# Three banks of scores in the first visit of each batch's first pair, the fourth bank behind the value products: local attention woven into a bilinear feed-forward on one NeuronCore

## The chip, the cores and the metric

The kernel runs on one core of one Trainium2 chip. The metric is the device time of one launch in microseconds (us). The time before is 975.85 us, the median of three runs (973.68 to 976.51).

## The reference

Eight batches of eight heads, 576 positions and head dimension 64 go through attention with a causal window of 128 and a linear distance bias; the result, 512 wide per position, goes through a bilinear feed-forward with inner width 1536.

```python
scores = scale * np.matmul(q, k.transpose(0, 1, 3, 2))
bias = slopes[:, None, None] * (-np.abs(rel).astype(np.float32))[None, :, :]
mask = (rel >= 0) & (rel < window)
scores = np.where(mask, scores + bias[None], -1000000000.0)
scores = scores - np.max(scores, axis=-1, keepdims=True)
attn = np.exp(scores)
attn = attn / (np.sum(attn, axis=-1, keepdims=True) + 1e-09)
attn_out = np.matmul(attn, v)
...
a = x @ w_a
b = x @ w_b
return (a * b @ w_out).astype(np.float32)
```

## The kernel before, in words

**Two interleaved streams.** The feed-forward of one batch is the main stream: `up` (two products with the inner weights, some of them as a seven-product scheme, `up_fast`) and then `down` (line 1003, 48 steps of six 128x288 matmuls, each with its own 128x128 weights). The attention of a later batch is a Python generator, `attention()`, that yields seven times per pair of heads; `Pace.along` advances it evenly along the main stream. Batches are numbered 0 to 7 here and pairs of a batch 0 to 3. Pair 0 and pair 1 of batch b run beside `down` of batch b-2, pairs 2 and 3 beside `up` of batch b-1. In the code `i` is the running pair, `p` its place in the batch, `o` the pair whose scores are made, `prev` the pair before it, `nxt` the next one, and `two` is 2 for batches 2 to 7.

**What sets the order.** From batch 1 of the feed-forward on, TensorE's instructions stand in the order in which the code issues them. The other engines' orders, and that of SyncE's queue of DMAs, are set by a scheduler that weighs due times, so a move on TensorE can reorder them too. Each engine then executes its own list strictly in order, waiting on semaphores. A run of attention matmuls between two steps of the main stream is called a visit below.

**One pair of attention.** `scores(o, bi)` makes one of four PSUM banks of scores (line 417: 128x64 weights `qst`, 192 columns; bank 0 holds three 64-row tiles of queries, banks 1 to 3 two each); VectorE adds the bias and takes the minimum (line 422), ScalarE the exponential (line 423) into a tile `t`. `normalize(o)` takes the reciprocal of the row sums (435, 436) and writes the probabilities as a 16-bit high part (ScalarE, 439) and low part (VectorE, 440) into `phl`. `transpose_probs` is one DMA transpose of `phl` into `pT` (445), issued by SyncE once both parts of all banks are there. `pv` multiplies `pT` with the split values `vhl` (541); ScalarE copies the result back over the values `v` (454). There is one buffer each of `phl`, `pT`, `qst`, `qk` and `v`, four of `t`, and three PSUM banks (`ps_at`) for scores, value products and small totals.

**The next pair's layout.** `split_qk(nxt)` and `low_qk(nxt)` split the loaded queries and keys into high (`qkh`, ScalarE 373) and low parts (`qkl`, VectorE 378), scaled by a factor `own` (VectorE 112, 118, 119, 371) that comes from one small matmul `qtot` (367). `lay_out_qk` moves them with four DMAs of SyncE's queue: 385 and 386 copy the upper halves into `qst`, then 387 and 388, which must wait for these to land, move the lower halves. Scores of a pair need all four.

**The values.** When pair 0 of a batch runs, the batch before is finished: `split_x` (POOL 489 to 499, ScalarE 475, VectorE 476) reads the whole of `v` to make the feed-forward's input, `hidden_scale` (TensorE 556, VectorE 557) finds its scale. Only then `load_v` (SyncE 297, 1280 KB) may fill `v` for the new batch, in pair 1. `v_squares` takes its squares, two of four parts on ScalarE (309), two on VectorE (307).

Of the kernel before, what the change touches and what calls it, by code (L numbers as in the profile page):

```python
# [46 lines left out]
def attention_then_bilinear_ffn(ctx: ExitStack, tc: tile.TileContext, qT, kT, vP, w_a, w_b, w_out, rel, slopes2, outT):  # L47
# [245 lines left out]
    def load_v(b):  # L293

        st = State()
        st.v = work.tile([P, NPAIR, VCOLS], F32, tag="v", name="v")
        sp.dma_start(st.v, vP[b])
        st.xq = work.tile([P, S], BF16, tag="xq", name="xq")
        return st
# [49 lines left out]
    def qk_squares(b, p, qk):  # L349
        o = State()  # L350
        o.b, o.p, o.qk = b, p, qk
        sums = small.tile([P, 1], F32, tag="qs", name="qs")
        hi = work.tile([P, 2, S], F16, tag="qkh", name="qkh", bufs=2)
        lo = work.tile([P, 2, S], F16, tag="qkl", name="qkl", bufs=2)
        with tc.issue_after(last_phl[0].ins) if b == 2 and p == 1 else ExitStack():
            act.activation(lo.bitcast(BF16), qk, AF.Square, accum_out=sums)

        o.both = small.tile([P, 2], BF16, tag="both", name="both")
        o.ready = vec.tensor_scalar(out=o.both, in0=halves, scalar1=sums, scalar2=None, op0=ALU.mult)
        o.kh, o.kl = hi, lo  # L360
        return o

    def split_qk(o):

        b, p, qk, hi, lo = o.b, o.p, o.qk, o.kh, o.kl
        tot = ps_at.tile([P, 512], F32, tag="at", name="qtot")
        pe.matmul(tot[:, 0:2], ones16, o.both, start=True, stop=True)
        sc = small.tile([P, 2], F32, tag="sc", name="sc")
        power_scale(sc, tot[:, 0:2], 1.01, 15)
        own = small.tile([P, 3], F32, tag="own", name="own")  # L370
        vec.tensor_tensor_reduce(out=own[:, 0:2], in0=sc, in1=halves, scale=1.0, scalar=0.0, op0=ALU.mult, op1=ALU.add, accum_out=own[:, 2:3])
        own = own[:, 2:3]
        act.activation(hi, qk, AF.Copy, scale=own)
        o.sc, o.own = sc, own

    def low_qk(o, behind=None):
        with tc.issue_after(behind.ins) if behind else ExitStack():
            vec.scalar_tensor_tensor(out=o.kl.rearrange("p h s -> p (h s)"), in0=o.qk.rearrange("p h s -> p (h s)"), scalar=o.own, in1=o.kh.rearrange("p h s -> p (h s)"), op0=ALU.mult, op1=ALU.subtract)
# [17 lines left out]
    def before_scores(o, ninv):  # L396
        o.bias = work.tile([P, WIN], F32, tag="bias", name="bias")
        last_bias[0] = pool.tensor_scalar(out=o.bias, in0=rel_sb, scalar1=ninv, scalar2=sl2_sb[:, o.p:o.p + 1], op0=ALU.mult, op1=ALU.mult)  # L398
        o.mn, o.sm, o.rin = (small.tile([P, 9], F32, tag=tag, name=tag) for tag in ("mn", "sm", "rin"))
        o.n, o.parts = 0, []  # L400
# [26 lines left out]
    def normalize(o):  # L427

        a, z = o.parts[0][0], o.n

        if o.b < 2:
            vec.tensor_scalar(out=o.rin[:, a:z], in0=o.sm[:, a:z], scalar1=1e-9, scalar2=1.0 / PSC, op0=ALU.add, op1=ALU.mult)
        else:

            act.activation(o.rin[:, a:z], o.sm[:, a:z], AF.Copy, scale=1.0 / PSC, bias=1e-9 / PSC)
        vec.reciprocal(o.rin[:, a:z], o.rin[:, a:z])  # L436
        for m, e, pc, w in o.parts:
            s = o.rin[:, m:m + 1]
            beside[0] = last_phl[0] = act.activation(phl[:, 0, pc:pc + w], e, AF.Copy, scale=s)  # L439
            beside[1] = vec.scalar_tensor_tensor(out=phl[:, 1, pc:pc + w], in0=e, scalar=s, in1=phl[:, 0, pc:pc + w], op0=ALU.mult, op1=ALU.subtract)  # L440
        o.parts = []
# [102 lines left out]
    def pv(p, st, o, vhl):  # L544
        xp = new_x_ps()
        hi, lo = o.pT[:, 0:NCOL // P, :], o.pT[:, NCOL // P:2 * NCOL // P, :]
        each_pv(xp, (vhl[:, 0, :], vhl[:, 1, :], vhl[:, 0, :]), (hi, hi, lo))
        keep_x(p, st, xp, 1.0 / PSC)
# [161 lines left out]
    def attention():  # L710


        n = NPAIR * (B - 1)
        qks = {}

        def load(i):
            if i < n:

                qks[i] = (load_plain_qk if i < NPAIR else load_qk)(1 + i // NPAIR, i % NPAIR)

        def squares(i):
            if i >= n:
                return None
            qk = qks.pop(i)
            return qk if i < NPAIR else qk_squares(1 + i // NPAIR, i % NPAIR, qk)

        def split(o, whole=True):
            if o and o.b > 1:
                split_qk(o)
                if whole:  # L730
                    low_qk(o)

        def lay_out(o):
            if o:
                before_scores(o, lay_out_qk(o) if o.b > 1 else -8.0)

        def behind():

            return tc.issue_after(last_read[0].ins) if last_read[0] else ExitStack()

        load(0)
        st, prev = load_v(1), None
        o = squares(0)
        lay_out(o)
        load(1)
        yield 0
        for i in range(n + 1):
            b, p = 1 + i // NPAIR, i % NPAIR

            two = 2 if o and o.b >= 2 else 1  # L750
            if two == 2 and p == 1:
                with behind():
                    nxt = squares(i + 1)
            for bi in range(two if o else 0):
                scores(o, bi, nxt.ready if two == 2 and p == 1 and nxt else None)
            if two == 1 or p != 1:
                with behind():
                    nxt = squares(i + 1)
            if p == 1 and b > 1:
                st = load_v(b)  # L760
            if p == (1 if b == 1 else 2):
                v_scale(st)
            yield i + 1 / 7
            if o and two == 1:
                scores(o, 1)

            if p == 2:

                with tc.issue_after(first_reads[0].ins) if first_reads[0] else ExitStack():
                    late.vhl = split_v(st, late.p)  # L770
            elif prev and p != 1:
                prev.vhl = split_v(st, prev.p)
            yield i + 2 / 7
            if p == 2:
                pv(late.p, st, late, late.vhl)
                transpose_probs(prev)
                split(nxt)
            if o and p != 2:
                with behind():
                    normalize(o)  # L780
            if p != 2:
                split(nxt, p != 3)
            yield i + 3 / 7
            if o:
                scores(o, 2)
            if p == 3 and nxt and nxt.b > 1:
                low_qk(nxt, beside[1])
            if prev and p not in (1, 2):
                pv(prev.p, st, prev, prev.vhl)
            if two == 2 and p in (1, 3):  # L790
                if p == 2:
                    with behind():
                        normalize(o)
                scores(o, 3)
            yield i + 4 / 7
            if p == 2:
                prev.vhl = split_v(st, prev.p)
                if two == 1 or p not in (1, 3):
                    with behind():
                        normalize(o)  # L800
            if o and (two == 1 or p not in (1, 3)):
                scores(o, 3)
            lay_out(nxt)
            load(i + 2)
            if p == (0 if b == 1 else 1):
                v_squares(st, (0, 1))
            if prev and p == 0:
                states[b - 1] = st
                assert started["down"] == b - 2
                for k, _ in enumerate(split_x(st, b - 1 <= 3, b - 1 >= 2)):  # L810
                    yield i + (4.2 + 0.2 * k) / 7
            yield i + 5 / 7
            if o:
                with behind():
                    normalize(o)
            if p == (0 if b == 1 else 1):
                v_squares(st, (2, 3), vec if b > 2 else act)
            yield i + 6 / 7
            if prev and p == 0:
                hidden_scale(st)  # L820
            if p == 2:
                pv(prev.p, st, prev, prev.vhl)
            if p == 1:
                late = prev
            elif o:
                transpose_probs(o)
            prev, o = o, nxt
            yield i + 1
# [305 lines left out]
```

## Time and profile before

| what | value |
|---|---|
| runs before | 973.68, 975.85, 976.51 us |
| the profiled execution's own time | 975.07 us |
| its span, first to last instruction | 973.3 us |
| outside the span | 1.8 us |
| TensorE busy | 958.6 us, 98% of the span |
| VectorE busy | 683.1 us |
| ScalarE busy | 626.3 us |
| POOL busy | 260.7 us |
| mean granted TensorE clock | 0.996 |

A line of the timeline gives start, duration, engine, source line, operation, the tiles written and read, and a count; a bracket gives idle time just before it and what ended that. PE is TensorE, PEld its weight loads, DVE VectorE, ACT ScalarE, SPq SyncE's queue of DMAs. A line of the waits gives the waiting engine and line, what it waited for, the total in us, the number of times and the longest.

### The profile page before, as it was taken

To read this page: it belongs to the slowest core of one execution; us is meant where nothing else is said; L and a number is where in the kernel's file an instruction comes from. 1 tells how busy PE (TensorE), PEld (TensorE's weight loads), DVE (VectorE), ACT (ScalarE), POOL (GpSimd) and SP (SyncE) were. 2 spreads that over 40 slices of the span, in tenths; PEclk is the share of its full clock that TensorE was granted. 3 is DMA by queue.
4 is the path that set the end of the run, shared out by engine and by line. 5 is a ranking of instruction groups with operands and counts; after the bars stand their busy time and mean duration, and the time that the engine had idled before them with its cause. 6 is when DMAs were issued, how large, how long until landed. Compare 5 with 4: busy or idle time off the path is not lost.

```text
span 973.3 us, 23844 instructions
## 1 busy us (share of the span) xinstructions
PE 958.6 (98%) x9340; PEld 747.8 (77%) x9341; DVE 683.1 (70%) x1896; ACT 626.3 (64%) x1701; POOL 260.7 (27%) x307
## 2 busy tenths in 40 slices
PE   8989999999999999999999999999999999999998
PEld 6667777777877777777877777777777778877776
DVE  6999998568888768887777877667676676514520
ACT  6878788577776666776766876767666765423321
POOL 1211122044546123631235222401222122301100
PEclk9999999999999999999999999999999999999999
DMA  9463736635347333464246552464245450210001
GB/s 351 143 259 111 254 84 135 146 102 111 90 97 171 75 69 72 109 158 93 52 92 172 101 104 50 111 177 93 45 94 130 117 100 12 57 37 2 1 13 37
DMA packets 148432, 102.82 MB, mean 106 GB/s; under 512 B 120032, under 2 KB 128352, under 8 KB 147296
## 3 DMA queue, kind: packets, MB, share of 16 engines
q1 hardware_dynamic: 138816, 91.77, 38.5%
q10 hardware_dynamic: 9504, 9.54, 3.1%
q8 instruction: 73, 1.20, 0.5%
q14 instruction: 39, 0.32, 0.1%
HBM read 48.33 MB, written 9.44 MB: 59 GB/s over the span
## 4 chain that ended last, share of the span: by engine, by line
PE 86%; DVE 5%; DMA 4%; ACT 3%; issue 1%; SPq 0%; POOL 0%; ACTq 0%; DVEq 0%
PE dn_ps L1003 23%; PE ch L907 19%; PE up_ps L907 17%; PE p L907 15%; PE x_ps L541 5%; PE sc_ps L417 4%; DMA v<-in_vP 2%; PE dn_ps L869 1%; PE sc_ps L413 1%; DMA pT<-phl 1%; DMA wdn<-in_w_b 1%; ACT vsq L309 1%; DVE phl L440 1%; DVE vsq L307 0%; DVE xs L476 0%
## 5 line engine op out<-in xcount | busy, mean ns | idle before, releaser
L907 PEld LDWEIGHTS <-wup 128*128 128x128 f16 x3072 | 296.5, 98 | 84.4 <-issue 7.9
L1003 PE MATMUL dn_ps<-h,wdn 128*128 128x288 f16 x2016 | 253.9, 286 | 0.0
L1003 PEld LDWEIGHTS <-wdn 128*128 128x128 f16 x2016 | 194.0, 98 | 51.8
L907 PE MATMUL up_ps<-xs,wup 128*128 128x288 f16 x1536 | 196.6, 287 | 2.8 <-DVE v L670 2.1
L962 POOL TENSOR_TENSOR rc<-rc,row 128x288 f32<-128x288 f32 x64 | 61.8, 966 | 275.1 <-DVE row L960 259.2
L907 PEld LDWEIGHTS <-wsum 128*128 128x128 f16 x1152 | 111.7, 98 | 30.9 <-issue 1.3
L423 ACT ACTIVATE t<-t,mn 128x192 f32<-128x192 f32 (+2 forms) x252 | 107.2, 427 | 26.4 <-DVE mn L422 26.2
L440 DVE SCALAR_TENSOR_TENSOR phl<-t,rin,phl 128x192 f16<-128x192 f32 (+2 forms) x252 | 107.1, 466 | 15.1 <-ACT phl L439 14.8
L907 PE MATMUL p<-xs,wup 128*128 128x288 f16 x768 | 115.0, 286 | 0.0
L907 PE MATMUL ch<-xs,wup 128*128 128x288 f16 x768 | 115.0, 286 | 0.0
L907 PE MATMUL ch<-xs,wsum 128*128 128x288 f16 x768 | 111.5, 286 | 0.4 <-ACT rc L932 0.4
L439 ACT ACTIVATE phl<-t,rin 128x192 f16<-128x192 f32 (+2 forms) x252 | 88.9, 425 | 29.2 <-DVE rin L436 15.6
L899 ACT CAST h<-rc 128x576 f16<-128x576 f32 x96 | 64.0, 668 | 63.1 <-DVE rc L967 38.1
L900 DVE TENSOR_TENSOR h<-rc,h 128x576 f16<-128x576 f32 x90 | 69.2, 770 | 29.8 <-ACT h L899 29.0
L422 DVE CUSTOM_DVE_ANT_0 t<-sc_ps,bias,neg 128x192 f32<-128x192 f32 (+2 forms) x216 | 73.6, 389 | 10.1 <-PE sc_ps L417 10.0
L1008 ACT ACTIVATE row<-dn_ps,oi 128x288 f32<-128x288 f32 x56 | 27.7, 494 | 57.3 <-PE dn_ps L1003 57.3
L476 DVE TENSOR_TENSOR xs<-v,xs 128x576 f16<-128x576 f32 x52 | 48.0, 934 | 22.5 <-ACT xs L475 22.4
L944 ACT ACTIVATE row<-ch,g 128x288 f32<-128x288 f32 x64 | 31.8, 498 | 49.0 <-PE ch L907 48.9
L398 POOL TENSOR_SCALAR bias<-rel_sb,ninv,sl_sb 128x192 f32<-128x192 f32 x24 | 23.9, 995 | 139.1 <-DVE mn L422 121.1
L939 DVE TENSOR_TENSOR rc<-p,rc 128x288 f32<-128x288 f32 x64 | 29.1, 454 | 44.4 <-PE p L907 34.8
L907 PE MATMUL p<-xs,wsum 128*128 128x288 f16 x384 | 57.5, 286 | 0.0
L967 DVE SCALAR_TENSOR_TENSOR rc<-rc,g,ch 128x288 f32<-128x288 f32 x64 | 32.6, 510 | 23.7 <-PE ch L907 23.6
(158 smaller groups left out, 1381.0 us busy)
## 6 DMA issues: line engine op xcount, KB each, us to landing
v<-in_vP SPq DMA_DIRECT2D x8, 1280.0 KB, 6.2
out<-row ACTq DMA_DIRECT2D x62, 144.0 KB, 1.8
qk<-in_qT SPq DMA_DIRECT2D x28, 288.0 KB, 4.0
qk<-in_kT SPq DMA_DIRECT2D x28, 288.0 KB, 4.4
wdn<-in_w_a SPq DMA_DIRECT2D x12, 512.0 KB, 5.2
wdn<-in_w_b SPq DMA_DIRECT2D x12, 512.0 KB, 6.1
wdn<-in_w_out SPq DMA_DIRECT2D x12, 512.0 KB, 5.0
qst<-qkh SPq DMA_DIRECT2D x24, 144.0 KB, 2.8
```

The source lines that it names most:

```text
L417: pe.matmul(ps[64 * e:64 * e + 64, c:c + w], o.qs[:, e, qq], ks[:, e, kk], start=not last, stop=last)
L422: beside[1] = vec.tensor_tensor_reduce(out=t[:, c:c + w], in0=ps[:, c:c + w], in1=o.bias[:, WIN - w:WIN], scale=-0.125 if o.b == 1 else o. ...
L423: beside[0] = act.activation(t[:, c:c + w], t[:, c:c + w], AF.Exp, bias=o.mn[:, n:n + 1], scale=-1.0, accum_out=o.sm[:, n:n + 1])
L439: beside[0] = last_phl[0] = act.activation(phl[:, 0, pc:pc + w], e, AF.Copy, scale=s)
L440: beside[1] = vec.scalar_tensor_tensor(out=phl[:, 1, pc:pc + w], in0=e, scalar=s, in1=phl[:, 0, pc:pc + w], op0=ALU.mult, op1=ALU.subtract)
L476: vec.tensor_tensor(out=xs[:, n, 1, :, :], in0=src, in1=xs[:, n, 0, :, :], op=ALU.subtract)
L541: last = pe.matmul(xp[oc // 512][64 * h:64 * h + 64, o0:o0 + w], vt[0:rows, c:c + 64], probs(pt, rows, blocks, h), start=(n == 0 and first ...
L899: act.copy(h[:, f, :, 0, :], hid)
L900: eng.tensor_tensor(out=h[:, f, :, 1, :], in0=hid, in1=h[:, f, :, 0, :], op=ALU.subtract)
L907: pe.matmul(ps[:, 0:HT], w[:, wi, k, :], xs[:, b, xi, k, :], start=(first and n == 0), stop=(last and n == len(ks) - 1), skip_group_check= ...
L962: pool.tensor_tensor(out=x0, in0=x0, in1=mid, op=ALU.mult)
L1003: pe.matmul(ps[:, 0:HT], wdn[:, f, wi, e * P:(e + 1) * P], h[:, f, t, hi, :], start=(m == 0 and n == 0), stop=(m == NF - 1 and n == 2))
```

## The change

For pair 0 of batches 2 to 7, three banks of scores are made in the first visit instead of two; the third visit, which held bank 2 and the value products of the pair before, now holds the value products and then bank 3, and the visit that held bank 3 alone is gone. `normalize(o)`, whose places in the code stay, therefore handles seven tiles at its first call (five before) and two at its second (four before). Other pairs keep their order in the code.

```diff
-            for bi in range(two if o else 0):
+            for bi in range((3 if two == 2 and p == 0 else two) if o else 0):
                 scores(o, bi, nxt.ready if two == 2 and p == 1 and nxt else None)
...
-            if o:
+            if o and (two == 1 or p):
                 scores(o, 2)
             if p == 3 and nxt and nxt.b > 1:
                 low_qk(nxt, beside[1])
             if prev and p not in (1, 2):
                 pv(prev.p, st, prev, prev.vhl)
-            if two == 2 and p in (1, 3):
-                if p == 2:
-                    with behind():
-                        normalize(o)
+            if o and two == 2 and p != 2:
                 scores(o, 3)
             yield i + 4 / 7
...
-            if o and (two == 1 or p not in (1, 3)):
+            if o and (two == 1 or p == 2):
                 scores(o, 3)
             lay_out(nxt)
```

The file is three lines shorter, so that lines behind the change have numbers three lower (1003 becomes 1000).

On TensorE, at the end of the value products in pair 0 of batch 6, the main stream followed before:

```order
L541 LDWEIGHTS vhl
L541 MATMUL x_ps<-pT,vhl 64x64
L541 LDWEIGHTS vhl
L541 MATMUL x_ps<-pT,vhl 64x64
L1003 LDWEIGHTS wdn
L1003 MATMUL dn_ps<-h,wdn 128x288
```

and now eight matmuls of scores stand there first, of which four are shown:

```order
L541 LDWEIGHTS vhl
L541 MATMUL x_ps<-pT,vhl 64x64
L417 LDWEIGHTS qst
L417 MATMUL sc_ps<-qkh,qst 64x192
L417 LDWEIGHTS qst
L417 MATMUL sc_ps<-qkh,qst 64x192
L417 LDWEIGHTS qst
L417 MATMUL sc_ps<-qkl,qst 64x192
L417 LDWEIGHTS qst
L417 MATMUL sc_ps<-qkl,qst 64x192
```

Bank 3 has moved up by 18 matmuls of the main stream, and bank 2, which stood ahead of the value products, is now in the visit before.

On SyncE's queue, between pair 0 and pair 1 of batch 6, the transpose of the probabilities stood ahead of the load of the values before:

```order
L387 DMA qkh<-qkh 64x1152
L388 DMA qkl<-qkl 64x1152
L445 DMA_TRANSPOSE pT<-phl 128x32x128
L297 DMA v<-in_vP 128x2560
L385 DMA qst<-qkh 64x1152
L386 DMA qst<-qkl 64x1152
```

and now:

```order
L387 DMA qkh<-qkh 64x1152
L388 DMA qkl<-qkl 64x1152
L346 DMA qk<-in_kT 64x2x576
L297 DMA v<-in_vP 128x2560
L445 DMA_TRANSPOSE pT<-phl 128x32x128
L385 DMA qst<-qkh 64x1152
L386 DMA qst<-qkl 64x1152
```

The two have changed places, in batch 7 as well; in batches 2 to 5 the transpose stays first.

On VectorE, in pair 1 of batch 6 (first half of its scores, then the factor `own` for the next pair, then the normalization), before:

```order
L436 RECIPROCAL rin<-rin 128x5
L112 TENSOR_SCALAR cl<-qtot 128x2
L118 TENSOR_SCALAR r<-cl 128x2
L119 TENSOR_SCALAR sc<-r 128x2
L371 ISA own<-sc,halves 128x2
L371 ISA own 128x1
L440 SCALAR_TENSOR_TENSOR phl<-t,rin,phl 128x64
```

and now:

```order
L307 ISA vsq,vs<-v 128x640
L307 ISA vs 128x1
L112 TENSOR_SCALAR cl<-qtot 128x2
L436 RECIPROCAL rin<-rin 128x5
L307 ISA vsq,vs<-v 128x640
L307 ISA vs 128x1
L118 TENSOR_SCALAR r<-cl 128x2
L440 SCALAR_TENSOR_TENSOR phl<-t,rin,phl 128x64
L440 SCALAR_TENSOR_TENSOR phl<-t,rin,phl 128x128
L314 CAST vc_10225<-vs 128x4
L119 TENSOR_SCALAR sc<-r 128x2
L440 SCALAR_TENSOR_TENSOR phl<-t,rin,phl 128x192 x2
```

The squares of the new values have moved ahead of this work, and `own` (371, in the next row there) behind four of the five low parts of the probabilities. The split 378 has moved behind the four rows of line 422 of the second half of the scores. ScalarE's order in the same pair has both its squares (309) ahead of the reciprocal sums and the high parts, where they stood behind 373 before. Batch 7 is the same as batch 6.

## The prediction

> **What bounds the kernel now.** I read the page first (span, busy time, chain), then the waits of TensorE, then the timeline around one changed pair.
>
> ```profile
> span 973.3 us, 23844 instructions
> PE 958.6 (98%) x9340; PEld 747.8 (77%) x9341; DVE 683.1 (70%) x1896; ACT 626.3 (64%) x1701; POOL 260.7 (27%) x307
> PE 86%; DVE 5%; DMA 4%; ACT 3%; issue 1%; SPq 0%; POOL 0%; ACTq 0%; DVEq 0%
> ...
> PE sc_ps L417 <- DMA qkh<-qkh: 0.8, 1, 0.8
> PE up_ps L907 <- ACT rc L918: 0.4, 1, 0.4
> ...
> PEld L417 <- issue: 13.9, 55, 1.1
> ...
> ACT phl L439 <- DMA pT<-phl: 11.8, 7, 2.9
> ACT vsq L309 <- DMA v<-in_vP: 9.3, 7, 1.9
> ```
>
> TensorE is busy 98% of the span and holds 86% of the chain; the other engines are below 71%. So the time moves only by what TensorE does differently: turns between main stream and visits, and waits. Its listed waits on other engines or DMAs are a few tenths each; the weight loads of scores, on the other hand, have 55 gaps that wait for nothing shown, 13.9 us in all, 0.25 each on average. Those are the turns. The last two rows are off TensorE, but they are where this change presses: high parts waiting for a transpose, squares waiting for the values.
>
> **The turns: minus 1.3 us.** TensorE in pair 0 of batch 6, from bank 2 to bank 3:
>
> ```profile
> 622.16 0.25 PE L417 MATMUL sc_ps<-qkl,qst 128*64 128x192 f16 x2
> 622.24 1.51 PE L541 MATMUL x_ps<-pT,vhl 128*64 128x128 f16 x42
> 623.69 2.38 PE L1003 MATMUL dn_ps<-h,wdn 128*128 128x288 f16 x18
> 626.00 0.27 PE L417 MATMUL sc_ps<-qkh,qst 128*64 128x192 f16 x2
> 626.10 0.25 PE L417 MATMUL sc_ps<-qkl,qst 128*64 128x192 f16 x2
> 626.18 0.25 PE L417 MATMUL sc_ps<-qkh,qst 128*64 128x192 f16 x2
> 626.27 0.25 PE L417 MATMUL sc_ps<-qkl,qst 128*64 128x192 f16 x2
> 626.45 0.54 PE L1003 MATMUL dn_ps<-h,wdn 128*128 128x288 f16 x3
> ```
>
> The 18 matmuls follow each other by (2.38 - 0.29)/17 = 0.123, where 0.29 is how long one stays in the pipe (its records overlap). A nineteenth would have come at 623.69 + 18 x 0.123 = 625.90; the scores came at 626.00: 0.10 lost going in. Pairs of score matmuls follow by 0.08 (0.10 the first time), so the main stream could resume at 626.35 and did at 626.45: 0.10 lost going out. From scores to value products (622.16 to 622.24) nothing is lost beyond the 0.08. Merging a visit that holds one bank into others therefore saves 0.10 + 0.02 + 0.10 = 0.22. The same matmuls run, eight per bank, on both sides of the change. Six pairs x 0.22 = 1.3. Its bounds are near: 1.2 to 1.4.
>
> What covers the moved work: the third bank needs the third PSUM bank, last read in the pair before; its two evictions (0.4 each on VectorE) and exponentials (0.44 each on ScalarE) fill the roughly 2 us that these engines idle there before the first normalization. If that cover went, the first `normalize` would slip, and with it the high part 373 and copies 454, which TensorE needs only in pair 1. I cost it at nothing.
>
> **The wait in batch 5: minus 1.0 us.** In pair 2 of batch 5 TensorE waits for the layout:
>
> ```profile
> 540.70 0.90 PE L907 MATMUL ch<-xs,wup 128*128 128x288 f16 x6
> 542.38 0.22 PE L417 MATMUL sc_ps<-qkh,qst 128*64 128x64 f16 x2 [0.78 <-DMA qkh<-qkh]
> 542.86 0.22 PE L417 MATMUL sc_ps<-qkl,qst 128*64 128x64 f16 x2 [0.27 <-DVE phl L440]
> ```
>
> The brackets make 1.05 us. That layout begins in pair 1 behind a normalization which itself waits for the transpose of pair 0. With only two tiles of pair 0 left for its second `normalize`, that transpose goes out earlier in batch 5, and in the new order the two layout DMAs 387 and 388 also stand ahead of the load of `qk`, not between. I expect the wait to go, 1.0 of 1.05; at worst it stays, 0.
>
> **What is late next: plus 2.1 us in batches 6 and 7.** There the queue's order changed: the load of the values (297) now stands ahead of the transpose (445). Before, in batch 6:
>
> ```profile
> 635.20 4.71 SPq L445 DMA_TRANSPOSE pT<-phl  x1
> 640.01 0.61 SPq L297 DMA_DIRECT2D v<-in_vP  x1
> 644.99 0.47 SPq L385 DMA_DIRECT2D qst<-qkh  x1
> 646.45 0.46 SPq L386 DMA_DIRECT2D qst<-qkl  x1
> ...
> 648.77 0.46 SPq L388 DMA_DIRECT2D qkl<-qkl  x1
> ```
>
> ```profile
> 642.15 1.68 ACT L439 ACTIVATE phl<-t,rin 128x64 f16<-128x64 f32 x5 [1.99 <-DMA pT<-phl]
> 643.73 1.24 ACT L373 ACTIVATE qkh<-qk,own 128x1152 f16<-128x1152 f32 x1
> 646.04 0.74 ACT L309 ACTIVATE vsq<-v 128x640 bf16<-128x640 f32 x1 [1.07 <-DMA v<-in_vP]
> ```
>
> So the transpose took 642.15 - 635.20 = 6.95 from issue to landing, the values 646.04 - 640.01 = 6.03, and both together, from 635.20 to 646.04, 10.84, with the DMA engines nearly full (share 0.94, second figure from the right):
>
> ```profile
> 635.20:646.05 10.85, 10.85 (x109) 8.47 (x104) 6.99 (x32) 6.18 (x21) 0.00 (x0) 1.00 0.94 247
> ```
>
> When are they issued after the change? The values may be loaded once `split_x` has read `v`:
>
> ```profile
> 624.90 1.41 POOL L492 TENSOR_TENSOR v<-v 128x576 f32<-128x576 f32 x1 [10.08 <-ACT v L454]
> 631.10 1.41 POOL L499 TENSOR_TENSOR v<-v 128x576 f32<-128x576 f32 x1
> ...
> 631.06 0.67 ACT L475 CAST xs<-v 128x576 f16<-128x576 f32 x1 [0.86 <-POOL v L494]
> 635.10 0.74 DVE L476 TENSOR_TENSOR xs<-v,xs 128x576 f16<-128x576 f32 x1
> ```
>
> POOL's chain of five ends at 632.51 before; two exponentials that stood between the copies 454 are gone, so about 0.5 earlier, 632.0; then one cast of 0.67 and one subtraction of 0.74, which no longer queues behind low parts: `v` is free at 633.4 instead of 635.84. The transpose, behind the last two low parts (0.4 each), is ready at about 634.6 instead of 635.20, but stands behind the values. If the pair of transfers again needs 10.84 from its first issue, now with the transpose last, it lands at T = 633.4 + 10.84 = 644.2 instead of 642.15.
>
> From T to the scores of pair 2:
>
> ```profile
> 643.17 1.11 DVE L440 SCALAR_TENSOR_TENSOR phl<-t,rin,phl 128x192 f16<-128x192 f32 x3
> 645.00 1.42 DVE L378 SCALAR_TENSOR_TENSOR qkl<-qk,own,qkh 128x1152 f16<-128x1152 f32 x1 [0.73 <-ACT qkh L373]
> ...
> 647.35 0.41 DVE L422 CUSTOM_DVE_ANT_0 t<-sc_ps,bias,neg 128x192 f32<-128x192 f32 x1
> 647.69 0.08 DVE L422 DVE_READ_ACCUMULATOR2_ANT mn<- 128x1 f32 x1
> ...
> qst<-qkl SPq DMA_DIRECT2D x24, 144.0 KB, 2.7
> qkl<-qkl SPq DMA_DIRECT2D x24, 144.0 KB, 2.5
> ...
> 654.33 0.22 PE L417 MATMUL sc_ps<-qkh,qst 128*64 128x64 f16 x2
> 654.38 0.20 PE L417 MATMUL sc_ps<-qkl,qst 128*64 128x64 f16 x2
> ```
>
> Before, 378 ended at 646.42, 4.3 behind T, and its last DMA (388) landed at about 648.77 + 2.5 = 651.3, 3.1 ahead of the need at 654.38. After, `own` stands behind the fourth low part: T + 1.8 (643.17 + 0.74 - 642.15) plus some 0.4 of small operations, T + 2.2. Then the fifth low part and two small ones (0.7), then four evictions at 0.34 (1.4): 378 starts at T + 4.3, later than 373 lets it (T + 2.2 + 1.24), and ends at T + 5.7. Then 386 lands 2.7 later, T + 8.5 with its issue, and 388, which waits for that, lands 2.5 later: T + 11.0. The need is at 654.38 - 0.22 = 654.16, so T must be 643.1 or less. T = 644.2 costs 1.05; twice, 2.1. ScalarE is not later than this: with the values landing at 633.4 + 6.03 = 639.4, its two squares (0.9 each) still leave it ready before T.
>
> The ends: the transpose at its own pace, 634.6 + 6.95 = 641.5, costs nothing; the transpose only after the values are through, 633.4 + 6.03 + 6.95 = 646.4, costs 3.3 each, 6.6 in all. I take the shared pace because it is the measured one for exactly these two.
>
> One rule of the Trainium skill, in its page "DMA: Bandwidth & Descriptors", section "Queues, rings and completion order", speaks against the change: on each DMA engine descriptors of one issuing queue are consumed in the order of the ring, so a transpose issued behind the 1280 KB starts behind them. By that rule the sum would be near the upper end. The trace bears it out in part: the values, issued before the transpose had landed, took 6.03 and not 2.1 more.
>
> **Batch 2: plus 0.2 us.** Pair 1 of batch 2 runs beside `up`, whose PSUM banks ScalarE must empty (918). Two squares move ahead of that copy and may wait for the values. Before, TensorE lost 0.4 there (0.6 with the pipe); a later copy could make it 1.9, an earlier one nothing: minus 0.6 to plus 1.3. I take plus 0.2, near the middle. In batches 3 and 4 the transpose stays first and the layout has over 1 us to spare: nothing.
>
> **The sum.** -1.3 - 1.0 + 2.1 + 0.2 = 0.0. The profiled execution, 975.07 = span 973.3 + 1.8 outside, stays there; it lies 0.8 below the median 975.85, which I forecast as 975.9. About 0.3% (2.9 us) is what a measurement of this kernel can tell from no change.
>
> **Rivals.**
> - *No new wait.* T is 643.1 or less, since transfers of different kind share the engines well: -1.3 - 1.05 - 0.6 to -1.3 - 1.0 + 0.2, so 972.9 to 973.7. For it: the transpose's issue itself takes 4.7 us, so it spreads. Against it: the DMA share of 0.94. Chance 0.28, of which 0.11 passes 0.3%.
> - *The transpose is served strictly behind the values.* T = 646.4; from T = 645.4 on (2.3 per batch) with batch 2's upper end this decides for slower. Sum -1.3 - 1.0 + 6.6 + 0.2 = +4.5: 980.3. Chance 0.25, of which 0.22 passes 0.3%. (It is what the page's rule above describes.)
> - *The wait in batch 5 stays,* because 378 there, too, has moved behind four evictions (1.4 later), and the gain of the earlier transpose is used up: 976.9. Chance 0.12, within 0.3%.
>
> **How the numbers follow.** The forecast has 0.35; with the parts of the rivals inside 0.3% "same" has 0.67, faster 0.11, slower 0.22. The range, 973.0 to 980.0, runs from no new wait to nearly the serial case and leaves out some 0.2.
>
> **What would show it.** Right: one visit fewer in each pair 0 (six fewer gaps of weight loads of scores), no bracket on line 417 in batch 5, brackets of about 1 us on `qkl` in pair 2 of batches 6 and 7, and high parts (439) of pair 1 there starting about 2 us later than now relative to the first visit. Wrong: if those high parts start earlier than now, the load does not hold up the transpose, and the kernel is faster by over 2 us; if TensorE stops at the totals of `hidden_scale` (556) or at value products, a cover I took for granted is gone.

## The result and the profile after

The changed kernel takes 986.93 us (984.43 to 987.52, five runs), the kernel before 975.4 us (973.68 to 976.51, five runs): 1.0107 times as long, 95% interval 1.0095 to 1.012, so slower and clear of the noise. The forecast was no change, 975.9, with a range up to 980.0. The profiled execution after is the shortest of its five, 984.43 us, with a span 9.0 longer than before; what follows accounts for these 9.0, and the other 2.5 of the medians' 11.5 are in no trace.

From the page after (span, busy time, shares of the chain):

```profile
span 982.3 us, 23843 instructions
PE 957.9 (98%) x9340; PEld 747.6 (76%) x9341; DVE 683.4 (70%) x1896; ACT 625.2 (64%) x1701; POOL 266.7 (27%) x307
PE 73%; DMA 9%; DVE 7%; ACT 6%; issue 2%; POOL 2%; SPq 1%; ACTq 0%; DVEq 0%; POOLq 0%
```

The work is the same, 957.9 us of TensorE against 958.6. What changed is the chain that ends last: TensorE had 86% of it and has 73%, DMAs went from 4% to 9%, and 13% lies on VectorE and ScalarE. The kernel waits more; it does not compute more. TensorE's waits after say where (waited for, us in total, times, longest), with the last row on the gaps of weight loads that wait for nothing shown. Left out are rows that both kernels have and rows of the first 160 us, where the order is the same; those differ too (at line 413, 2.0 against 0.6), but the main stream is only 0.1 behind there:

```profile
PE sc_ps L417 <- DMA qkl<-qkl: 3.8, 4, 2.3
PE ch L904 <- ACT row L941: 2.1, 3, 1.7
...
PE up_ps L904 <- ACT rc L915: 1.9, 2, 1.0
...
PE n_ps L556 <- POOL xq L470: 1.6, 1, 1.6
...
PE up_ps L904 <- DVE rc L917: 0.7, 1, 0.7
...
PE ch L904 <- DVE rc L964: 0.2, 1, 0.2
...
PEld L417 <- issue: 10.7, 45, 0.2
```

These six rows make 10.3 us. Before, the waits in the same stretch were 0.8 and 0.3 for the layout (417) and 0.4 for the copy of `up`: 1.5. So 8.8 us of new waits, in nine more stops; each stop costs some 0.17 beyond its bracket (worked out below from one in batch 3), 1.5 in all; and the six turns saved give 1.3 back. 8.8 + 1.5 - 1.3 = 9.0, the difference of the spans. (The gaps of weight loads of scores fell from 55 to 45 and from 13.9 to 10.7, more than six visits account for: they are not turns alone. The turns are measured below by the main stream itself.)

Batch by batch the new waits have four places. **Batch 2, 2.6 us:** ScalarE stands at a square of the values (309) that is not yet loaded, and the copy of `up_ps` that TensorE needs (915) comes late. ScalarE's and TensorE's rows:

```profile
196.00 0.74 ACT L309 ACTIVATE vsq<-v 128x640 bf16<-128x640 f32 x1 [3.38 <-DMA v<-in_vP]
202.87 0.38 ACT L915 COPY rc<-up_ps 128x288 f32<-128x288 f32 x1
203.30 1.63 PE L904 MATMUL up_ps<-xs,wup 128*128 128x288 f16 x12 [1.04 <-ACT rc L915]
```

The exponentials of bank 1, the high parts and two copies (915) queue behind that square and the next ones. The middle one of the three stops ends with VectorE's copy (917); ahead of the last, ScalarE's square of q and k (356) had waited 1.79 for its load. **Batch 3, 1.6 us:** GpSimd's queue after (POOL in the rows), and the stop of TensorE that follows from it:

```profile
288.06 1.71 POOL L398 TENSOR_SCALAR bias<-rel_sb,ninv,sl_sb 128x192 f32<-128x192 f32 x1
289.74 3.07 POOL L267 TENSOR_TENSOR wsum<-wup 128x512 f32<-128x512 f16 x2
292.77 1.38 POOL L470 TENSOR_TENSOR xq<-xq,sq 128x576 bf16<-128x576 bf16 x1
...
287.82 4.82 PE L1000 MATMUL dn_ps<-h,wdn 128*128 128x288 f16 x38
294.21 0.41 PE L556 MATMUL n_ps<-xq,ones 128*128 128x512 bf16 x2 [1.57 <-POOL xq L470]
```

The sum of squares (470) stands behind the bias and two sums of weights. Before it stood ahead of them:

```profile
286.56 1.28 POOL L470 TENSOR_TENSOR xq<-xq,sq 128x576 bf16<-128x576 bf16 x1 [1.12 <-ACT sq L469]
```

(The 38 matmuls start every 0.1225, (4.82 - 0.29)/37, so the last starts at 292.35 and the next should have at 292.47; it started at 294.21. The stop cost 1.74, 0.17 more than its bracket.) **Batch 5, 1.9 us instead of 1.05:** ScalarE, SP's queue and TensorE:

```profile
537.27 0.74 ACT L309 ACTIVATE vsq<-v 128x640 bf16<-128x640 f32 x1 [2.54 <-DMA v<-in_vP]
538.01 1.24 ACT L373 ACTIVATE qkh<-qk,own 128x1152 f16<-128x1152 f32 x1
...
543.01 0.46 SPq L388 DMA_DIRECT2D qkl<-qkl  x1
...
544.28 0.64 SPq L346 DMA_DIRECT2D qk<-in_kT  x1
...
548.99 1.16 ACT L356 ACTIVATE qkl<-qk 128x1152 bf16<-128x1152 f32 x1 [2.63 <-DMA qk<-in_kT]
...
552.28 0.90 PE L904 MATMUL ch<-xs,wup 128*128 128x288 f16 x6 [1.67 <-ACT row L941]
```

A square of the values stands ahead of the high half 373. So 373 is late, the layout is late, the loads of the next `qk` behind it are late, ScalarE waits 2.63 for them at 356, and the `row` that TensorE needs stands behind 356. The wait at the visit itself has fallen to 0.25. **Batches 6 and 7, 1.3 and 2.5 us:** SP's queue, ScalarE, and TensorE in batch 6, with TensorE in batch 7 as the last row; then, from issue to landing, the two DMAs of batch 6 and those of batch 7:

```profile
638.44 0.35 SPq L297 DMA_DIRECT2D v<-in_vP  x1
639.70 7.40 SPq L445 DMA_TRANSPOSE pT<-phl  x1
...
645.30 0.74 ACT L309 ACTIVATE vsq<-v 128x640 bf16<-128x640 f32 x1 [2.44 <-DMA v<-in_vP]
649.16 1.68 ACT L439 ACTIVATE phl<-t,rin 128x64 f16<-128x64 f32 x5 [0.95 <-DMA pT<-phl]
660.10 0.22 PE L417 MATMUL sc_ps<-qkl,qst 128*64 128x64 f16 x2 [0.91 <-DMA qkl<-qkl]
...
774.46 0.22 PE L417 MATMUL sc_ps<-qkl,qst 128*64 128x64 f16 x2 [2.31 <-DMA qkl<-qkl]
```

```profile
v<-in_vP SPq DMA_DIRECT2D x1, 1280.0 KB, 6.8
pT<-phl SPq DMA_TRANSPOSE x1, 9.4
...
v<-in_vP SPq DMA_DIRECT2D x1, 1280.0 KB, 8.0
pT<-phl SPq DMA_TRANSPOSE x1, 10.5
```

The transpose, now behind the 1280 KB of values, lands 9.4 and 10.5 after its issue, against 6.9 and 7.8 before.

### The profile page after: what moved, and what is told of

The parts are those of the page before. It is cut to its first block, busy times and chain, and to the rows that moved or that the text cites. A ratio compares the mean times of both kernels' runs of the same rounds, so it can differ in the third digit from the quotient of the medians.

```text
span 982.3 us, 23843 instructions
## 1 busy us (share of the span) xinstructions
PE 957.9 (98%) x9340; PEld 747.6 (76%) x9341; DVE 683.4 (70%) x1896; ACT 625.2 (64%) x1701; POOL 266.7 (27%) x307
## 4 chain that ended last, share of the span: by engine, by line
PE 73%; DMA 9%; DVE 7%; ACT 6%; issue 2%; POOL 2%; SPq 1%; ACTq 0%; DVEq 0%; POOLq 0%
PE ch L904 18%; PE up_ps L904 15%; PE dn_ps L1000 15%; PE p L904 13%; PE x_ps L541 4%; DMA v<-in_vP 3%; DMA qk<-in_kT 3%; PE sc_ps L417 3%; PE dn_ps L866 2%; DMA qst<-qkl 1%; ACT t L423 1%; PE sc_ps L413 1%; ACT vsq L309 1%; DVE xs L476 1%; DVE phl L440 1%
## 5 line engine op out<-in xcount | busy, mean ns | idle before, releaser
L440 DVE SCALAR_TENSOR_TENSOR phl<-t,rin,phl 128x192 f16<-128x192 f32 (+2 forms) x252 | 105.2, 459 | 10.3 <-ACT phl L439 9.9
L476 DVE TENSOR_TENSOR xs<-v,xs 128x576 f16<-128x576 f32 x52 | 51.1, 995 | 19.3 <-ACT xs L475 19.1
L475 ACT CAST xs<-v 128x576 f16<-128x576 f32 x52 | 34.6, 667 | 24.4 <-POOL v L494 14.0
```

The source lines that it names most:

```text
L475: act.copy(xs[:, n, 0, :, :], src)
L476: vec.tensor_tensor(out=xs[:, n, 1, :, :], in0=src, in1=xs[:, n, 0, :, :], op=ALU.subtract)
```

## The experiments

The theory after this reading: the change of TensorE's program is a small gain, and the loss comes from the orders of the other queues, which the scheduler set anew. The rival: TensorE's new program itself, three banks in a row, crowds the engines that serve it. Each of the first runs puts one order back by an edge in the schedule, with TensorE's program left as changed; `tc.issue_after(x)` puts what follows behind `x` in its queue.

**The sum of squares first (e1).**

```diff
-            pool.tensor_tensor(out=st.xq, in0=st.xq, in1=sq, op=ALU.add)
+            last_xq[0] = pool.tensor_tensor(out=st.xq, in0=st.xq, in1=sq, op=ALU.add)
...
+        with (tc.issue_after(last_xq[0].ins) if o.b > 1 and o.p == 1 ...):
             last_bias[0] = pool.tensor_scalar(out=o.bias, ...
```

> The changed kernel, with one order put back: on GpSimd the bias of pair 1 (398) stands behind the last addition of squares (470) again, in every batch. TensorE's program is unchanged. Theory A (the loss comes from the other engines' queues, whose order moved with the change): the wait of 1.6 us at the totals of hidden_scale (556) in batch 3 goes, nothing else does; 985.3 where the changed kernel takes 986.9. Rival B (the loss comes from TensorE's own new program: three banks in a row crowd the evictions, the copies of the value products and their squares): the squares would still be summed late, the wait at 556 stays within 0.3 us, 986.9.

Measured: 983.23 us, 1.0082 of the kernel before (1.0067 to 1.0098). The wait at 556 is gone, and a smaller one stands 10 us later in batch 3, at the total of `qk`; the row of TensorE's waits:

```profile
PE qtot L367 <- DVE both L359: 1.3, 1, 1.3
```

Batch 5's two waits are gone as well, which was not expected: there the values landed 6.4 us after issue instead of 7.7, and the square ahead of 373 hardly held it up. It goes with this edge: in the five runs that hold the sum first (e1, e4, e8, e9, e10) the values of batch 5 took 6.1 to 6.4, in the six changed programs without it 7.3 to 8.0, before 6.7. By what path GpSimd's order reaches that load stays open. The order on GpSimd is shown to be the cause of the wait at 556; rival B is out for this place.

**The values behind the transpose (e2).**

```diff
-        sp.dma_start(st.v, vP[b])
+        with (tc.issue_after(last_tp[0].ins) if b > 1 ...): sp.dma_start(st.v, vP[b])
```

> The changed kernel, with the load of the values (297) put behind the transpose of pair 0 (445) on SP's queue again; in batches 6 and 7 the scheduler then also puts ScalarE's squares of the values (309) back behind the high parts, as before the change. Theory A: the waits for the layout (417, 0.9 and 2.3 us in batches 6 and 7) and the 0.2 to 0.4 us behind them at rows go, batches 2 to 5 keep theirs: about 3.8 less, 983.1. Rival B (TensorE's own program): the waits stay, 986.9.

Measured: 980.26 us, 1.005 (1.0035 to 1.0066). No wait of batches 6 and 7 over 0.2 us is left; those of batches 2, 3 and 5 stay (1.25, 0.70 and 0.49; 1.60; 0.24 and 1.80). The gain in the medians, 6.7, is larger than the 3.8 expected; between the profiled executions it is 4.9. The edge moves the squares of batches 6 and 7 too, as said ahead, so this run alone does not part the two.

**The squares behind the high parts (e3).**

```diff
-                v_squares(st, (0, 1))
+                with (tc.issue_after(last_phl[0].ins) if b > 1 ...): v_squares(st, (0, 1))
```

> The changed kernel, with ScalarE's first two squares of the values (309) held behind the high parts (439) of pair 1's first normalization in all batches, as they stood before; on SP the values (297) stay ahead of the transpose (445) in batches 6 and 7. Both readings take back batch 2 (the copies 915 no longer stand behind squares that wait for values): about 2.2 us. Reading A1 (batches 6 and 7 are late because the transpose is served behind 1280 KB of values): their waits on the layout stay, 0.9 and 2.3 within 0.5; 984.7. Reading A2 (they are late because ScalarE stands still at the squares and the exponentials behind them come late): those waits go too, another 3.2; 981.5.

Measured: 986.8 us, 1.0116 (1.0102 to 1.013). Batch 2's three waits are gone, as both readings had it. Against A2, batches 6 and 7 keep a wait: ScalarE no longer stands at a square and is idle before the high parts until the transpose lands, as A1 has it. A1's figure holds in batch 6 (0.74) but not in batch 7 (1.02 instead of 2.3 within 0.5): the load of q (345), which stood ahead of the copy 388, stands behind it here, and that copy landed 2.6 after its issue instead of 3.8. The time is 2.1 above A1's. ScalarE in batch 6:

```profile
648.19 1.68 ACT L439 ACTIVATE phl<-t,rin 128x64 f16<-128x64 f32 x5 [5.21 <-DMA pT<-phl]
```

Missed was a new loss. In all three of batches 5, 6 and 7 one square stood between the high parts and 373 (in batch 5 as before this edge), and the late loads of `qk` held up the row:

```profile
PE ch L904 <- ACT row L941: 6.0, 3, 2.2
PE sc_ps L417 <- DMA qkl<-qkl: 2.3, 4, 1.0
```

What batch 2 gave came back there. So the next run puts the squares behind 373.

**The squares behind the high half of q and k (e5).**

```diff
-        act.activation(hi, qk, AF.Copy, scale=own)
+        last_hi[0] = act.activation(hi, qk, AF.Copy, scale=own)
...
-                v_squares(st, (0, 1))
+                with (tc.issue_after(last_hi[0].ins) if b > 1 ...): v_squares(st, (0, 1))
```

> The changed kernel with ScalarE's first two squares of the values (309) held behind the high half of q and k (373) of pair 1 in all batches (in the run that held them behind the high parts 439 alone, one square still stood ahead of 373). On SP the load of the next q (345) thereby goes back between the two halves of the layout; the values stay ahead of the transpose in batches 6 and 7. Theory (in batch 5, and in the earlier run in batches 6 and 7, 373 waits behind a square that waits for the values; so the layout, then the loads of q and k, then the squares 356 and the row 941 are late): batch 2's waits and the 1.7 at the row 941 of batch 5 go, rows in batches 6 and 7 stay under 0.5, the waits for the layout there stay at 0.7 to 2.3, the one at 556 stays 1.6: 982.4 where the changed kernel takes 986.9. Rival (only the landing of the values, or of q and k themselves, is late, whatever stands before 373): the row waits stay within 0.4 of 1.7 in batch 5, 984.3.

Measured: 979.23 us, 1.0034 (1.0021 to 1.0047); 3.2 better than expected. TensorE's waits that are left of the new ones:

```profile
PE sc_ps L417 <- DMA qkh<-qkh: 2.7, 2, 1.8
...
PE n_ps L556 <- POOL xq L470: 1.5, 1, 1.5
...
PE sc_ps L417 <- DMA qkl<-qkl: 1.2, 3, 0.5
```

Batches 2 and 5 wait no more; batches 6 and 7 still wait for the layout (1.5 and 2.3) with no square ahead of 373, batch 3 at 556. The values of batch 5 landed no sooner (8.0 after issue), so the theory of batch 5 holds against its rival.

**Only the load put back in batch 5's layout (e6).** SP's queue in pairs 1 by edges between these DMAs; 373 stays behind a square. The block gives the order of the queue, not code; in batches 6 and 7, too, 345 moves, from behind 387 to ahead of it.

```diff
         # SP's queue, pair 1 of batches 3 and 5
-        385 386 387 388 345 346
+        385 386 345 387 388 346
```

> The changed kernel with one order put back on SP alone: in pairs 1 the load of the next q (345) stands between the two halves of the layout (behind 386, ahead of 387) and that of k (346) behind 388, as before the change; 373 still stands behind a square. If the row wait in batch 5 (1.7 us) is mainly that the loads were put behind all four layout DMAs: k is issued 0.8 us earlier, the wait falls to about 0.9; 986.1. If it is mainly the late 373 (theory of the run above): also no more than that, and it stays above 0.8. If the loads' place were all of it, it falls under 0.3; 985.3.

Measured: 984.94 us, 1.01 (1.0086 to 1.0114). The row wait of batch 5 is gone and the time is near 985.3, as the last reading had it (the loads' place is all of it). But that reading is not the answer, because the visit before it now waits; TensorE, then the last two layout DMAs of this run from issue to landing, then the same two of the changed kernel:

```profile
546.41 0.22 PE L417 MATMUL sc_ps<-qkh,qst 128*64 128x64 f16 x2 [1.27 <-ACT wup L277]
547.17 0.22 PE L417 MATMUL sc_ps<-qkl,qst 128*64 128x64 f16 x2 [0.54 <-DMA qkl<-qkl]
```

```profile
qkh<-qkh SPq DMA_DIRECT2D x1, 144.0 KB, 4.4
qkl<-qkl SPq DMA_DIRECT2D x1, 144.0 KB, 4.3
```

```profile
qkh<-qkh SPq DMA_DIRECT2D x1, 144.0 KB, 2.5
qkl<-qkl SPq DMA_DIRECT2D x1, 144.0 KB, 2.8
```

1.81 at the visit instead of 1.92 in two places: the load of `q` between the copies makes them land 1.9 and 1.5 later, the load behind them lands late itself. In batch 5 either order is paid; together with the run above, which puts the load in the same place and 373 ahead of the squares, this leaves the late 373 as the root. (The first bracket names ScalarE's cast, which had long been done; it is the copy `qkh<-qkh` that landed last, issued at 541.88 and 4.4 on the way.)

**All old orders (e4).** The three edges above (squares behind 373, values behind the transpose, bias behind the sum), and further ones (lines with # tell an order in words):

```diff
+        # pairs 1, SP: 385 386 345 387 388 346, as in the run above
+        # pair 1, VectorE: squares (307) behind low_qk (378)
-                scores(o, 2)
+                scores(o, 2, last_low[0] if two == 2 and p == 1 else None)   # evictions behind low_qk
```

> The changed kernel's TensorE program (three banks in the first visit, the fourth behind the value products) with the orders of the other queues held as before the change: the bias behind the last addition of squares, the values behind the transpose, the squares of the values behind the high half of q and k, the evictions of pair 1's last banks behind the low half, the load of q between the two halves of the layout. Theory A: all new waits go and the six turns of 0.22 remain as a gain: 975.4 - 1.3 = 974.1 where the kernel before takes 975.4; the wait of 1.05 in batch 5 may stay or go, so 973.0 to 975.4. Rival B (TensorE's own program): most of the waits stay, 980 or more.

Measured: 974.67 us, 0.9989 of the kernel before (0.998 to 0.9997). Theory A holds: with the old orders the same program of TensorE is no loss but a small gain, 1.1. That this is near the 1.3 of the turns is chance. In the traces the main stream gains 1.3 by the turns, 0.6 in batch 2 and 1.3 in batch 5, where waits of the kernel before are gone, and loses 1.4 by a new wait at 367 in batch 3 (bracket 1.26) and 0.9 in batch 4 (0.6 at the layout in brackets).

**Three edges only (e9).** Without the further ones:

> The changed kernel's TensorE program with three orders held and nothing else: the bias (398) of pair 1 behind the last addition of squares (470), the values (297) behind the transpose (445), the squares of the values (309) behind the high half of q and k (373). If these three queues are all of the loss: the same as the run with all old orders, 974.7 within 0.8 where the kernel before takes 975.7, with the wait of 1.3 at the total of q and k (367) in batch 3 still there. If the evictions' and loads' places, held in that run too, had a part of their own: 976 or more.

Measured: 974.49 us, 0.9984 (0.9975 to 0.9993). Three orders are all of the loss of 11.5 us. The others follow from them: in the traces of e4 and e9 every engine and SP's queue run the same operations on the same tiles in the same order, so the two runs are one program measured twice.

**The fourth bank alone (e7).** Half of the change on TensorE:

```diff
-            for bi in range((3 if two == 2 and p == 0 else two) if o else 0):
+            for bi in range(two if o else 0):
...
-            if o and (two == 1 or p):
+            if o:
                 scores(o, 2)
```

> Half of the change on TensorE: in pair 0 of batches 2 to 7 the first visit holds two banks as before the change, the third stays in its visit with the value products, the fourth comes right behind them; the visit of one bank is gone all the same. Schedulers' orders follow by themselves: the values stand ahead of the transpose in batches 6 and 7 and the bias ahead of the sum of squares, as with the whole change, but batches 2 and 5 keep the order of the kernel before. Theory A (queues): the six turns (-1.3), the wait at 556 in batch 3 (+1.6), the waits for the layout in batches 6 and 7 (+3.8), none in batches 2 and 5: 975.7 + 4 = 979.7. Rival B (three banks in a row are what costs): no such waits, 974.4.

Measured: 983.74 us, 1.0086 (1.0072 to 1.01), 4 more than expected. No wait at 556, none in batch 2, 1.1 in batch 5 as before the change, batches 6 and 7 waiting as with the whole change. New is a wait in pair 0 itself, which neither theory had; TensorE's waits, and the place in batch 3 on TensorE and VectorE:

```profile
PE sc_ps L417 <- DVE mn L422: 3.9, 5, 1.1
```

```profile
283.22 0.27 PE L417 MATMUL sc_ps<-qkh,qst 128*64 128x192 f16 x2 [1.11 <-DVE mn L422]
...
281.07 1.42 DVE L378 SCALAR_TENSOR_TENSOR qkl<-qk,own,qkh 128x1152 f16<-128x1152 f32 x1 [0.73 <-ACT qkh L373]
282.41 0.41 DVE L422 CUSTOM_DVE_ANT_0 t<-sc_ps,bias,neg 128x192 f32<-128x192 f32 x1
```

Bank 2 and the value products take all three PSUM banks; the fourth bank of scores must wait until VectorE has emptied bank 2, behind its 378. With three banks in the first visit bank 2 is empty by then: that half of the change is no cost but what makes the other half possible. Rival B is out.

**A version that beats both (e8, then e10).** Of e4's remaining wait at 367, one guess was the loads of `qk` in pair 0, the other the place of ScalarE's square 356 behind a cast (475) that waits for GpSimd. The first guess, on top of all old orders:

```diff
+            if two == 2 and p == 0 and i + 2 < n:
+                load(i + 2)
+                with tc.issue_after(last_ld[0].ins): lay_out(nxt)
```

> As the run with all old orders, and also in pairs 0 the loads of the next q and k (345, 346) stand ahead of the layout (385 to 388) as before the change. There the last wait of size was 1.3 us at the total of q and k (367) in batch 3, behind ScalarE's square 356, which came late because its q and k were loaded late. Theory: that wait goes; 974.7 - 1.3 = 973.4, 0.997 to 0.998 of the kernel before. Rival: 356 is late by its place behind the casts (475) on ScalarE and not by the load; the wait stays, 974.7.

Measured: 975.19 us, 1.0 (0.9991 to 1.0009): the wait stays at 1.23, so the loads are not it. The other guess, on top of the three edges:

```diff
-        split(3, b21)
+        later.append(lambda: split(3, b21))
+        if len(states) != 3: later.pop()()
...
                     nxt = squares(i + 1)
+                with tc.issue_after(last_sq[0].ins) if later else ExitStack(): [f() for f in later]; later.clear()
```

> As the run with three pins, and in batch 3 the last cast of split_x (475, which waits for GpSimd's 499) behind ScalarE's square of q and k (356), as before the change. Theory: the wait of 1.3 us at 367 comes from 356 standing behind that cast; it falls under 0.3 and the kernel takes 1.0 to 1.3 less than with three pins alone: 973.5. Rival: 356 is then still late, because its q and k land late; the wait stays over 0.8, 974.6.

Measured: 972.29 us, 0.9969 of the kernel before (0.9958 to 0.998), 2.2 less than with three edges. The wait at 367 is gone, and the main stream gains 1.4 there; the rest is not shown to come from this edge, because the two profiled executions are 1.9 apart already at 160 us, where both run the same lists (the edge first acts at 292). ScalarE without the edge (first two rows, the run with all old orders) and with it:

```profile
296.07 0.67 ACT L475 CAST xs<-v 128x576 f16<-128x576 f32 x1 [2.91 <-POOL v L499]
...
297.65 1.16 ACT L356 ACTIVATE qkl<-qk 128x1152 bf16<-128x1152 f32 x1
```

```profile
293.08 1.16 ACT L356 ACTIVATE qkl<-qk 128x1152 bf16<-128x1152 f32 x1
...
295.10 0.67 ACT L475 CAST xs<-v 128x576 f16<-128x576 f32 x1 [0.76 <-POOL v L499]
```

## Why the prediction was wrong, step by step

- **The turns, -1.3: right.** Where no new wait lies, the same matmul of the main stream lags 0.22 to 0.23 less behind pair 0 than ahead of it (batch 3 from 2.37 to 2.14, batch 5 from 4.13 to 3.90, worked out from the starts in both traces). The gain of 1.1 to 1.4 with the queues put right (e4, e9) is not these turns alone (see the run e4).
- **Batch 5, -1.0: the failed step.** The wait at the visit did fall, from 1.05 to 0.25, but the prediction read the new place of 387 and 388 ahead of the load of `qk` only as a gain. It did not follow what was put behind them: 345 and 346, then 356, then the row. That is 1.67. It also passed over the new order on ScalarE, a square ahead of 373, which e5 and e6 show to be the root. The term was +0.9, not -1.0. The part on the transpose was right: it was issued 2.8 earlier against the main stream, and where the squares stand behind 373 (e4, e9) the wait of 1.05 does go.
- **Batches 6 and 7, +2.1: the delay right, its reason and the second size wrong.** The transpose behind the values delays the high parts and the layout, and A2, the obvious other reading, falls: with no square ahead of the high parts (e3) or of 373 (e5) the waits stay at 0.7 to 2.3. But the two transfers do not share a pace. The values are 128 packets of 10 KB, the transpose 4096 of 256 bytes. DMA packets of batch 6, before, from 635.2 to 641.5 and from 641.5 to 646.1; then after, from 638.44 to 643.5 and from 645.3 to 649.1:

```profile
DMA packets 4309, 1.25 MB, mean 199 GB/s; under 512 B 4138, under 2 KB 4308, under 8 KB 4308
DMA packets 253, 1.43 MB, mean 310 GB/s; under 512 B 38, under 2 KB 124, under 8 KB 124
...
DMA packets 123, 1.22 MB, mean 242 GB/s; under 512 B 1, under 2 KB 4, under 8 KB 4
DMA packets 3566, 0.93 MB, mean 244 GB/s; under 512 B 3539, under 2 KB 3566, under 8 KB 3566
```

The windows hold 1, 129, 119 and 0 packets over 8 KB (the 1, and one of the 129, are of another queue). Whichever is issued first is served first, and the other waits: after, 99 of the transpose's 4096 packets started before the last of the values did, and 2 in batch 7; before, none of the values' started ahead of the transpose's last in either batch. By the Trainium skill's page "DMA: Bandwidth & Descriptors", section "Queues, rings and completion order", descriptors of one queue are consumed in ring order on each DMA engine; the packets agree, in full and not "in part". The prediction's serial case, 12.98 (6.03 + 6.95), was mis-summed: it adds two times from issue to landing, though the second transfer is issued, and waits, while the first is served. (The first packet of the values came 1.9 after their issue behind the transpose, and 1.0 after it ahead.) Served one after the other, the pair takes the same time in both orders, 10.8 and 10.7 in batch 6. The rival "strictly behind the values" thus had the mechanism, at a wrong price, and the forecast the price with a wrong reason. So T came out as forecast (644.4, less the 4.65 by which the main stream lags there), and the wait was 0.91 for 1.05. The steps after T agree by luck: 386 landed 1.0 sooner than assumed, and 388 took 3.4 instead of the median 2.5. In batch 7 the wait was 2.31, because the pair takes 11.8 there (751.40 to 763.2), as it did before the change (746.70 to 758.47); the prediction used batch 6's numbers for both.
- **Batch 2, +0.2 (-0.6 to +1.3): the failed step.** The bound was taken from one copy of `up_ps` behind two squares. But a square that waits for a load holds up all of ScalarE's queue: exponentials, high parts and two such copies, 2.6 us in three stops against 0.42. With the squares behind the high parts (e3) or 373 (e5) all three stops are gone.
- **Costed at nothing: the moved work right, GpSimd's order wrong.** The third PSUM bank and the moved evictions cost nothing (e7 shows what lacking the bank costs). That the sum of squares moved behind the bias in batch 3 was in the order of the queue and was put at nothing without following it to the next thing that TensorE needs: 1.57. The prediction named a stop at 556 as what would make it wrong.
- **The sum.** Terms of -1.3, -1.0, +2.1, +0.2 and 0 were in truth about -1.3, +0.9, +3.9, +2.2 and +1.6 in brackets (batch 4 another 0.3), and 1.5 for the extra stops. No rival had this sum, because each rival varied one DMA, and three queues had changed. The forecast failed by these terms together, batch 2, batch 5, batch 3 and batch 7, and not by the sharing of two transfers, on which its range was built.

## What to carry to other kernels

When, as here, an engine that is never late is given a new program and the other queues are ordered by a scheduler, the new orders are the change: compare every queue, and for each instruction that moved ahead ask what it waits for and list all that stands behind it, up to the next thing that the bounding engine needs. Here a square that waited for a load stood ahead of work whose inputs were there, a long load ahead of a transpose that was needed first, and a bias ahead of a sum that TensorE waited for; three edges against these turned 1.0107 into 0.9984. And a wait that goes away is only gone when the next consumer of the same chain is shown to be on time.

## What the runs showed of the hardware

- Two transfers issued behind one another on SP's queue, a transpose of 4096 packets of 256 bytes and a load of 128 packets of 10 KB, were served in the order of issue, almost without overlap (rows above). The order did not change when the pair was through: 10.8 and 10.7 us from the first issue in batch 6, 11.8 both times in batch 7. It decided which of the two was late: over all runs the transpose of batches 6 and 7 landed 6.8 to 8.0 us after its issue when it was first and 8.6 to 11.0 when it was second. For the values the ranges overlap (5.8 to 7.3 as second, 6.1 to 8.0 as first).
- A 144 KB copy within the chip landed after 2.5 to 2.8 us with no load between (the changed kernel) and after 4.3 to 4.4 with a 288 KB load issued between it and its forerunner (e6).
- The same load of 1280 KB at the same place (batch 5) took 6.1 to 8.0 us between runs that differ only in the order of queues; it took 6.4 or less only where GpSimd's sum of squares stood first. What ran against it was not tried.
- A stop of TensorE cost about 0.17 us more than its bracket: 1.74 for 1.57 in batch 3 after the change, and 0.59 for the 0.42 of batch 2 before it, by what the main stream gained in e4 when that stop was gone.
